# Bf16 expert sums, late tiles in the dead transposed-x room, and another instruction order, in a fused local-attention and expert kernel

## Chip, cores, metric

The kernel runs on one core of one Trainium2 chip. The metric is device time in microseconds (us) for one execution. "Span" is the time from the first to the last instruction in a profiled execution; it is about 1.7 us shorter than the time. Engines: PE is TensorE, DVE is VectorE, ACT is ScalarE, POOL is GpSimd, SP is SyncE (here only a queue of DMA issues, "SPq"). Runs are "fast" or "slow"; a slow one is over 1.5% above the fastest of the same kernel. The "granted clock" is the share of its full clock that PE was allowed, and "DMA share" the mean busy share of the core's 16 DMA engines.

## The reference, cut to what matters

```python
x  = A_x                                   # 2048 tokens x 640, bf16
xn = layernorm(x)
q, k, v = split(xn @ wqkv)                 # 32 heads of 20
# each token attends to 8 keys: itself and 2, 4, ..., 14 tokens back
logits = einsum("bhsd,bhswd->bhsw", q, k[idx]) * scale      # masked where idx < 0
s  = einsum("bhsw,bhswd->bhsd", softmax(logits), v[idx]) @ wo
r  = xn @ w_r;  top 2 tokens by r go through an expert:
y  = (silu(x_sel @ w_gate) * (x_sel @ w_up)) @ w_down * sigmoid(r_sel)
g  = silu(xn with the two y's added at their tokens)
return x + s * g
```

## The kernel before

The 2048 tokens are four blocks of 512, j = 0 to 3. The work is cut into some 470 named steps, and a long string, ORDER, is the program order in which they are emitted. Each engine's own instructions come out near that order; the framework puts in the semaphores. Names that matter here: `xjg` is DVE's product q*k for block j from group g on (one group 4096 elements per partition, 2.29 us; two groups 8192, 4.4 us), `rjg` PE's reduction of it, `yjg` DVE's product attn*v, `ojgu` PE's reduction of that, `lb ex dn lg sb at` the softmax chain of PE and ACT, `s` output projections, `cm` DVE's combine with the gate, `od` POOL's accumulating store, `vs` the store of v, `vl` the gathers of shifted v, `kh` the key halo copy, `xr` the load of the last block's residual rows, `zo zw zi` the gate tiles' way through DRAM, `*` the 128x32 tiled form of a PE step (four times as many PE instructions), F4 a filler.

```python
k_sb = big.tile([P, KD, HALO + 2 * ST], BF)        # per group: 14 halo columns, even block, odd block

def key_halo():                                     # ACT: the odd block's last columns become the halo
    nc.scalar.copy(k_sb[:, :, 0:HALO], k_sb[:, :, 2 * ST:2 * ST + HALO])

def qk(j, gs):                                      # DVE: n groups at once
    koff = g * (HALO + 2 * ST) + HALO + ST * (j % 2)
    kv = bass.AP(k_sb.tensor, k_sb.offset + koff,
                 [[k_sb.ap[0][0], P], [HALO + 2 * ST, n], [-DIL, W], [1, ST]])
    nc.vector.tensor_tensor(out=dst, in0=q_sb[...].to_broadcast([P, n, W, ST]), in1=kv, op=ALU.mult)

def ss_tile(j):                                     # two rooms in turn for four blocks of s
    acc["ss", j] = ring.tile([P, TPS, D], BF, tag="ss", bufs=2)

def load_res():                                     # the last block's residual rows
    acc["xr"] = xr = ring.tile([P, TPS, D], BF, tag="we", name="xr")
    nc.sync.dma_start(xr[:], x2[ST * (NST - 1):S, :]...)

def gate_back():                                    # gate tiles back from DRAM, SyncE's queue too
    for k in range(2):
        dst, src = gate_tile(k)
        nc.sync.dma_start(out=dst, in_=src)

def expert_in(k):                                   # sums for the sigmoid, fp32 operands
    for i in range(2):
        nc.tensor.matmul(hp[:, FB:FB + 1], lhsT=srow[:, i, :], rhs=t8[:, i:i + 1], ...)
# ... (cut)
```

Of the kernel before, what the change touches and what calls it, by code (L numbers as in the profile page):

```python
# [8 lines left out]
BF = mybir.dt.bfloat16  # L9
F32 = mybir.dt.float32  # L10
# [45 lines left out]
x00d bh br x01d in x02d ls00 wq wk x03d ls01 W ls02 ls03 lv03 xd3 lv01 lp02 lp03 lz02 bi lz03 lp00 t02 lp01 te02  # L56
xd1 bn lz00 t03 lz01 te03 t01 ls32 t00 te01 q01b wv ls12 te00 q00b q01be k04 q00be q02a xd2 ls31 k00 q00a bm
q02ae k04e ls13 q04 mu3 mg5 ls11 k00e pr2 pr1 q00ae ls10 mg6 mg2 xw ls20 bs q03 ls33 lv33 lv31 q04e v02 ls30
q03e lp1 v02e v00 lz10 lz11 v01 lz12 v04 ls21 q02b v01e v00e lz13 t10 v03 k02 v04e x00 lv21 q02be te10 k01 ls23
v03e t12 k02e t13 r00 t11 vs0 k01e k03 te12 te13 lv23 x04 q01a ls22 lp3 lz31 te11 k14 q12 q01ae lp2 k11 lz32  # L60
k03e k10 k13 x02 lz22 k12 t22 q14 t31 q12e k11e k14e k10e k13e k12e q14e x03 x01 lz21 lz33 vh1 r01 te22 r02 lz20
r03 te31 vl01 vl02 r04 lb0 wc q13* q13e kh mg1 mu4 t33* mx0 mg3 v12 te33 ml0 t32 ng0 v12e lz30 x12 v14 t21 te32
ex0 vl00 lz23 q11 te21 v14e t20 te20 dn0 x11 q10 mg7 mu2 t23 q11e lg0 t30 sb0 v11 q10e v10 te23 v13 te30 q21 at0
x10 rt pr0 q22* r10 v11e v10e v13e m8 mi k21* r11 q23* vs1 g21 q22e g00 k23* g11 q21e k21e r12 k32* y00 k24* rr
g01 rm q23e mg4 lb1 o001 y01 k32e o001e vh2 o000 k24e q20* y02 mx1 k23e v20* k20* mg0 ix o011 v20e h0 q24* q20e
mu1 mu0 o011e ml1 k20e k22* hs o020 ng1* h1 v24* q24e o010 o000e wo1 wo3 k22e g10 wo2 k30* md1 md0 md4 x22 v22*
hb ex1 k30e x20 v24e dn1 k31 x21 lg1 o020e sb1 md2 v22e md3 k31e at1 wo0 v23 ht q30 v21 g31 v21e r20 q31* v23e
vs2 q33* g20 q31e g30 vl10 r21 q32* vl11 q30e y10 o010e r22 q33e q32e v33* o100 lb2 o101 q34* k33* vh3 mx2 v31*
q34e o101e hc ml2 k33e v31e y11 ng2* ex2 o100e o110 vl12 v32* v32e dn2 v34* vl20 lg2 sb2* at2 vl21 yp x30 y12
o111 zo r30 v33e zr v34e v30 s04 s03 v30e s02 vl22 x31 s01 s03e s00 s04e vs3 s01e o110e k34 zw o120 k34e s02e  # L70
o111e y20 o120e r31 xr x32 o200 s10* r32 zi y21 s12* s13* s00e vl30 lb3 mx3 ml3 y22 o200e vl31 cm0 ng3* s10e
s13e o201 s11* o211 ex3 dn3 od0 o201e lg3 s12e sb3* s14* at3 s11e y30 o211e s14e o220 o210 o220e o210e y34 vl32
cm1 y31 F4 o300 s20* s24* o340 s23 F4 s22 s21 o300e s23e s24e s20e o340e s22e s21e s33a o310 y32 o320 cm2 y35
o310e o320e od1 y33 s30* o350 od2 s31* o331 o330 o350e s30e s33b cm30 o331e o330e s32 s31e s32e cm33 cm31 od30
od33 cm32 od31 od32
# [25 lines left out]
def _build(ctx, tc, nc, A_x, A_wqkv, A_wo, B_w_r, B_w_gate, B_w_up, B_w_down, out):  # L101
# [39 lines left out]
    srow = big.tile([1, 2, P], F32, name="srow")  # L141
# [327 lines left out]

    def ss_tile(j):  # L470
        if ("ss", j) not in acc:
            acc["ss", j] = ring.tile([P, TPS, D], BF, tag="ss", bufs=2, name=f"ss{j}")
        return acc["ss", j]
# [46 lines left out]
    def load_res():  # L520
        acc["xr"] = xr = ring.tile([P, TPS, D], BF, tag="we", name="xr")
        nc.sync.dma_start(xr[:], x2[ST * (NST - 1):S, :].rearrange("(c p) d -> p c d", p=P))
# [71 lines left out]
    def route_merge():  # L594
# [8 lines left out]
        nc.vector.tensor_copy(ii[:], gi[:])  # L603

# [5 lines left out]
    def expert_in(k):  # L610
        hp = bank("pj", [P, FB + 1 - k], bufs=3, name="hp")
        if k == 0:
            for i in range(2):
                nc.tensor.matmul(hp[:, FB:FB + 1], lhsT=srow[:, i, :], rhs=t8[:, i:i + 1], start=(i == 0), stop=(i == 1))
# [193 lines left out]
```

## Time and profile before

| | before |
|---|---|
| time, median of the first 3 runs | 145.85 us (144.7 to 145.99) |
| span of the profiled run | 144.1 us |
| PE, DVE, ACT busy | 129.8, 117.7, 110.3 us |
| DVE's first weighting of values of block 1 (y10) starts | 84.72 us |
| from there to DVE's last instruction | 56.5 us, of which 3.7 waits |

The prediction below shows most of this profile. Four things it did not show proved to matter. First, the stages by tens of microseconds (us, then length, busy us of PE, PEld, DVE, ACT, POOL, granted clock, DMA share, GB/s), where 40 to 60 us is an undisturbed stretch:

```profile
40.00:50.00 10.00, 9.89 (x121) 5.95 (x112) 8.87 (x4) 9.76 (x19) 1.40 (x3) 1.00 0.60 145
50.00:60.00 10.00, 10.00 (x156) 4.78 (x158) 7.99 (x5) 9.05 (x12) 0.00 (x0) 1.00 0.46 147
```

Second, the key halo copy in ACT's instructions in order of time (start, us, engine, line, operation, out<-in). There is no bracket, so it waited for nobody:

```profile
41.34 0.25 ACT L343 COPY k_sb<-k_sb 128x70 bf16<-128x70 bf16 x1
```

The DMA queue by which instructions themselves come in (packets, MB, share of 16 engines), from the page:

```profile
q8 instruction: 15, 0.25, 0.8%
```

```profile
78.70 0.33 PE L184 MATMUL lg<-ld,nsel 128*128 128x128 bf16 x3 [0.68 <-issue]
...
98.49 0.77 PE L655 MATMUL yp<-wd,hT 128*32 128x160 bf16 x26 [0.63 <-issue]
```

### The profile page before, as it was taken

The numbers are of one execution on the slowest core, as the hardware profiler recorded it, in microseconds if no ns is written. First come the engines' busy times: TensorE is split into PE (matmuls) and PEld (weight loads), VectorE is DVE, ScalarE is ACT, GpSimd is POOL, SyncE is SP. The second block draws the span as 40 slices with busy tenths as digits, with TensorE's granted clock in tenths as the row PEclk, the third lists the DMA queues.
The fourth block names the chain that finished last, engine by engine and source line by source line (L and its number), as shares of the span: only waits on it lengthen the run. The fifth ranks groups of instructions, "written<-read, shape, count | busy, mean of one in ns | idle before, by whom it ended". The sixth has DMA issues, their size and how long they took to land.

```text
span 144.1 us, 4710 instructions
## 1 busy us (share of the span) xinstructions
PE 129.8 (90%) x1998; PEld 70.5 (49%) x2008; DVE 117.7 (82%) x112; ACT 110.3 (77%) x207; POOL 40.1 (28%) x130
## 2 busy tenths in 40 slices
PE   6959899999999999999997999997999888899740
PEld 2345445554565644545554454674644564645520
DVE  0563899899599758998168999999999997797971
ACT  3897999966699979996997989879258699164350
POOL 7888000047140000235500000551405057131200
PEclk9999999999999999999999999999999999999999
DMA  4999989629996024897999995798588979949682
GB/s 139 351 376 365 473 338 337 246 81 361 238 261 166 7 102 134 294 282 177 225 235 259 258 324 184 182 235 189 152 249 255 223 174 192 219 111 168 85 193 91
DMA packets 17516, 32.18 MB, mean 223 GB/s; under 512 B 2280, under 2 KB 14760, under 8 KB 16424
## 3 DMA queue, kind: packets, MB, share of 16 engines
q0 software_dynamic: 3888, 12.72, 39.5%
q1 hardware_dynamic: 10696, 16.15, 34.9%
q10 hardware_dynamic: 2912, 3.02, 6.4%
q8 instruction: 15, 0.25, 0.8%
q14 instruction: 5, 0.04, 0.1%
HBM read 26.24 MB, written 7.61 MB: 235 GB/s over the span
## 4 chain that ended last, share of the span: by engine, by line
PE 46%; DVE 20%; ACT 16%; DMA 11%; issue 3%; SPq 1%; POOL 1%; ACTq 0%; DVEq 0%
PE pp L184 21%; DVE prod L439 10%; DVE prod L363 8%; DMA z<-in_A_x_dram 7%; PE pp L187 7%; PE so L184 6%; ACT z L539 4%; DMA vsh<-vd 4%; ACT L169 3%; PE oa L454 3%; PE lg L374 2%; PE tp L192 2%; ACT k_sb L340 2%; ACT q_sb L333 2%; ACT o_sb L464 1%
## 5 line engine op out<-in xcount | busy, mean ns | idle before, releaser
L363 DVE TENSOR_TENSOR prod<-q_sb,k_sb 128x4096 bf16<-128x4096 bf16 (+1 forms) x14 | 44.6, 3201 | 7.9 <-PE oa L454 3.5
L355 POOL DMA_DIRECT2D vsh<-vd x48 | 24.3, 549 | 81.5 <-DMA vd<-v_sb 43.1
L439 DVE TENSOR_TENSOR prod<-attn,vsh 128x8192 bf16<-128x8192 bf16 (+4 forms) x15 | 44.6, 2994 | 2.1 <-DMA vsh<-vd 1.2
L184 PE MATMUL pp<-xnT,wqkv 128*128 128x512 bf16 (+1 forms) x188 | 41.1, 362 | 0.9 <-ACT q_sb L333 0.4
L187 PE MATMUL pp<-xnT,wqkv 128*32 128x512 bf16 x480 | 28.7, 379 | 0.1
L184 PEld LDWEIGHTS <-wqkv 128*128 128x128 bf16 x195 | 18.4, 98 | 18.7 <-issue 1.4
L187 PEld LDWEIGHTS <-wqkv 128*32 128x32 bf16 x480 | 13.3, 97 | 11.8 <-issue 0.4
L464 ACT CAST o_sb<-oa 128x512 bf16<-128x512 f32 (+2 forms) x22 | 11.9, 560 | 4.2 <-PE oa L454 4.2
L281 DVE BATCH_NORM_STATS2 st<-z 128x6 f32<-128x320 bf16 x20 | 8.6, 474 | 6.5 <-DMA z<-in_A_x_dram 6.4
L454 PE MATMUL oa<-prod,sall 128*32 128x512 bf16 (+2 forms) x240 | 12.0, 309 | 2.0 <-DVE prod L439 1.1
L333 ACT ACTIVATE q_sb<-pp 128x512 bf16<-128x512 f32 (+1 forms) x23 | 12.2, 543 | 2.0 <-PE pp L184 2.0
L340 ACT CAST v_sb<-pp 128x512 bf16<-128x512 f32 x20 | 11.4, 586 | 2.8 <-PE pp L184 1.7
L340 ACT CAST k_sb<-pp 128x512 bf16<-128x512 f32 x20 | 11.5, 590 | 2.6 <-PE pp L184 2.6
L169 ACT ACT_TABLE_LOAD x9 | 11.5, 1283 | 2.3 <-PEq L792 1.7
L487 ACT CAST ss<-so 128x512 bf16<-128x512 f32 x12 | 7.0, 596 | 7.0 <-PE so L184 7.0
L320 ACT COPY xnT<-tp 128x640 bf16<-128x640 bf16 x16 | 10.6, 696 | 0.4 <-PE tp L192 0.4
L374 PE MATMUL lg<-prod,ind 128*32 128x512 bf16 x160 | 10.6, 380 | 0.0
L539 ACT ACTIVATE z<-z 128x1280 bf16<-128x1280 bf16 x8 | 10.1, 1274 | 0.5 <-ACT v_sb L340 0.5
L184 PE MATMUL so<-wo,o_sb 128*128 128x512 bf16 (+1 forms) x54 | 8.9, 320 | 0.2 <-issue 0.2
L184 PEld LDWEIGHTS <-o_sb 128*128 128x128 bf16 x75 | 6.0, 98 | 6.0 <-ACT o_sb L464 0.6
L187 PEld LDWEIGHTS <-o_sb 128*32 128x32 bf16 x340 | 7.0, 97 | 4.0 <-ACT o_sb L464 0.7
L187 PE MATMUL so<-wo,o_sb 128*32 128x128 bf16 (+1 forms) x260 | 8.6, 281 | 0.0
(117 smaller groups left out, 140.5 us busy)
## 6 DMA issues: line engine op xcount, KB each, us to landing
vsh<-vd POOLq DMA_DIRECT2D x32, 262.6 KB, 5.4
vd<-v_sb ACTq DMA_DIRECT2D x4, 657.5 KB, 4.9
wqkv<-in_A_wqkv_dram SPq DMA_DIRECT2D x3, 800.0 KB, 13.1
wu<-in_B_w_up_dram SPq DMA_DIRECT2D x5, 432.0 KB, 4.1
vsh<-vd POOLq DMA_DIRECT2D x16, 131.1 KB, 6.6
z<-in_A_x_dram SPq DMA_DIRECT2D x3, 640.0 KB, 10.8
out_dram<-in_A_x_dram SPq DMA_DIRECT2D x3, 640.0 KB, 9.0
wd<-in_B_w_down_dram SPq DMA_DIRECT2D x4, 480.0 KB, 12.2
```

What stands on the lines that cost most here:

```text
L169: nc.scalar.preload_act_table_set(name)
L184: nc.tensor.matmul(dst, lhsT=lhsT, rhs=rhs, start=start, stop=stop, **kw)
L187: nc.tensor.matmul(dst[32 * c:32 * (c + 1)], lhsT=lhsT[:, 32 * c:32 * (c + 1)], rhs=rhs, start=start, stop=stop, tile_position=(0, 32 * c) ...
L333: nc.scalar.activation(out=dst, in_=pp[:], func=ACT.Copy, scale=SCALE)
L340: nc.scalar.copy(dst, pp[:])
L355: nc.gpsimd.dma_start(vsh[32 * i:32 * (i + 1), 4 * g0 * VR:4 * g0 * VR + n], src)
L363: nc.vector.tensor_tensor(out=dst, in0=q_sb[:, s0:s0 + n, :].unsqueeze(2).to_broadcast([P, n, W, ST]), in1=kv, op=ALU.mult)
L374: nc.tensor.matmul(lg[32 * w4:32 * (w4 + 1), w2, :], lhsT=ind5[:, g, :], rhs=prod[:, a:a + ST], start=(g == 0), stop=(g == G5 - 1), tile_p ...
L439: nc.vector.tensor_tensor(out=dst, in0=attn[:, :, t0:t0 + n].unsqueeze(2).to_broadcast([P, 2, 4 * ng, n]), in1=vv, op=ALU.mult)
L454: nc.tensor.matmul(oa[32 * dd:32 * (dd + 1), i, :], lhsT=sall[:, 0:32], rhs=prod[:, a:a + n], start=(w2 == 0), stop=(w2 == 1), tile_positi ...
L464: nc.scalar.copy(o_sb[:, s0:s0 + m, t0:t0 + n], acc.pop(("o", j, g, t0))[:])
L539: nc.scalar.activation(out=z[:, 2 * h:2 * h + 2, :], in_=z[:, 2 * h:2 * h + 2, :], func=ACT.Silu)
```

## The change

The intent: make the two sigmoid sums bf16 (fp32 multiplies are dearer on PE); put the s tiles of blocks 2 and 3 and the residual rows into the transposed x, which is dead after the last projection, so that they need not wait for the stores of blocks 0 and 1; drop one of two fillers; and use another order throughout. The diff, cut to its core:

```diff
 ORDER = """
-... lb0 wc q13* q13e kh mg1 mu4 t33* mx0 ... x12 ... x11 ... at0 x10 rt pr0 ...          (cut)
-... x22 v22* hb ex1 k30e x20 v24e dn1 k31 x21 ...                                        (cut)
+... q14* x11 x10 te30 kh te23 mg4 lb0 v11* ... ex0 ... lg0 sb0* rt v12e ...              (cut)
+... x20 h1 v24* v22e q24e o020 ... hb q30e x22 k31 ht ... x21 r21 hc y10 ...             (cut)
 """
-    srow = big.tile([1, 2, P], F32, name="srow")
+    srow = big.tile([1, 2, P], BF, name="srow")
+    t8b = big.tile([1, 2], BF, name="t8b")
+    def late_room(n):
+        return xnT[:].rearrange("p k s -> p (k s)")[:, n * TPS * D:(n + 1) * TPS * D]...
     def ss_tile(j):
-            acc["ss", j] = ring.tile([P, TPS, D], BF, tag="ss", bufs=2, name=f"ss{j}")
+            acc["ss", j] = ring.tile(...) if j < 2 else late_room(j - 2)
     def load_res():
-        acc["xr"] = xr = ring.tile([P, TPS, D], BF, tag="we", name="xr")
+        acc["xr"] = xr = late_room(2)
+        nc.vector.tensor_copy(t8b[:], t8[:, 0:2])
-                nc.tensor.matmul(hp[:, FB:FB + 1], lhsT=srow[:, i, :], rhs=t8[:, i:i + 1], ...)
+                nc.tensor.matmul(hp[:, FB:FB + 1], lhsT=srow[:, i, :], rhs=t8b[:, i:i + 1], ...)
```

More of the change, by code (lines that the diff above doesn't have):

```diff
@@ L55 @@
 ORDER = """
-x00d bh br x01d in x02d ls00 wq wk x03d ls01 W ls02 ls03 lv03 xd3 lv01 lp02 lp03 lz02 bi lz03 lp00 t02 lp01 te02
-xd1 bn lz00 t03 lz01 te03 t01 ls32 t00 te01 q01b wv ls12 te00 q00b q01be k04 q00be q02a xd2 ls31 k00 q00a bm
-q02ae k04e ls13 q04 mu3 mg5 ls11 k00e pr2 pr1 q00ae ls10 mg6 mg2 xw ls20 bs q03 ls33 lv33 lv31 q04e v02 ls30
-q03e lp1 v02e v00 lz10 lz11 v01 lz12 v04 ls21 q02b v01e v00e lz13 t10 v03 k02 v04e x00 lv21 q02be te10 k01 ls23
-v03e t12 k02e t13 r00 t11 vs0 k01e k03 te12 te13 lv23 x04 q01a ls22 lp3 lz31 te11 k14 q12 q01ae lp2 k11 lz32
@@ L61 @@
-k03e k10 k13 x02 lz22 k12 t22 q14 t31 q12e k11e k14e k10e k13e k12e q14e x03 x01 lz21 lz33 vh1 r01 te22 r02 lz20
-r03 te31 vl01 vl02 r04 lb0 wc q13* q13e kh mg1 mu4 t33* mx0 mg3 v12 te33 ml0 t32 ng0 v12e lz30 x12 v14 t21 te32
-ex0 vl00 lz23 q11 te21 v14e t20 te20 dn0 x11 q10 mg7 mu2 t23 q11e lg0 t30 sb0 v11 q10e v10 te23 v13 te30 q21 at0
-x10 rt pr0 q22* r10 v11e v10e v13e m8 mi k21* r11 q23* vs1 g21 q22e g00 k23* g11 q21e k21e r12 k32* y00 k24* rr
-g01 rm q23e mg4 lb1 o001 y01 k32e o001e vh2 o000 k24e q20* y02 mx1 k23e v20* k20* mg0 ix o011 v20e h0 q24* q20e
@@ L66 @@
-mu1 mu0 o011e ml1 k20e k22* hs o020 ng1* h1 v24* q24e o010 o000e wo1 wo3 k22e g10 wo2 k30* md1 md0 md4 x22 v22*
-hb ex1 k30e x20 v24e dn1 k31 x21 lg1 o020e sb1 md2 v22e md3 k31e at1 wo0 v23 ht q30 v21 g31 v21e r20 q31* v23e
-vs2 q33* g20 q31e g30 vl10 r21 q32* vl11 q30e y10 o010e r22 q33e q32e v33* o100 lb2 o101 q34* k33* vh3 mx2 v31*
-q34e o101e hc ml2 k33e v31e y11 ng2* ex2 o100e o110 vl12 v32* v32e dn2 v34* vl20 lg2 sb2* at2 vl21 yp x30 y12
-o111 zo r30 v33e zr v34e v30 s04 s03 v30e s02 vl22 x31 s01 s03e s00 s04e vs3 s01e o110e k34 zw o120 k34e s02e
@@ L71 @@
-o111e y20 o120e r31 xr x32 o200 s10* r32 zi y21 s12* s13* s00e vl30 lb3 mx3 ml3 y22 o200e vl31 cm0 ng3* s10e
-s13e o201 s11* o211 ex3 dn3 od0 o201e lg3 s12e sb3* s14* at3 s11e y30 o211e s14e o220 o210 o220e o210e y34 vl32
-cm1 y31 F4 o300 s20* s24* o340 s23 F4 s22 s21 o300e s23e s24e s20e o340e s22e s21e s33a o310 y32 o320 cm2 y35
-o310e o320e od1 y33 s30* o350 od2 s31* o331 o330 o350e s30e s33b cm30 o331e o330e s32 s31e s32e cm33 cm31 od30
-od33 cm32 od31 od32
+x00d x02d in x01d bh ls00 W x03d ls01 bi bm br lv01 ls02 ls03 lv03 lp02 lp03 bs lz02 xd1 lp00 t02 lp01 te02 lz03
@@ new lines @@
+lz00 lz01 t03 t00 wq t01 te03 te00 q01b ls10 q02b wv te01 ls11 q04 ls12 xd3 q01be v01 q02a ls13 q04e q02be lp1
+wk bn v01e mg7 q02ae ls31 v02 ls32 lv31 q00a q00ae v03 q00b lz12 lz11 v02e pr0 mg2 lz13 v03e lz10 q00be mg0 ls33
+k00 k00e v00 v00e q03 t10 k02 q03e ls30 q01a te10 k01 k02e q01ae lv33 t13 k03 t12 k04 xd2 mg6 mg3 t11 x00 k01e
+mu3 mu0 te13 lp3 k03e te12 te11 v04 k11 k04e ls20 x03 k14 k10 v04e q10 xw mg1 x01 vs0 ls23 k14e q11 k11e pr1 x02
+k13 k10e ls21 q13 q11e lv21 ls22 k12 vl02 lz33 t33 q10e k13e mg5 mu4 q12 lv23 x04 lz30 r00 wc q13e r01 r02 lp2
@@ new lines @@
+lz22 lz31 t22* r03 k12e lz32 lz23 te33 lz20 lz21 t30* t23* q12e r04 te22 vh1 q14* x11 x10 te30 kh te23 mg4 lb0
+v11* q14e mx0 vl01 vl00 t32 t31 v11e t21 ml0 ng0 v13 t20 te32 te31 te21 ex0 v12 v13e dn0 v10* te20 lg0 sb0* rt
+v12e v14* m8 v10e r10 r11 mi at0 x12 k22 g21 g11 k32 v14e rr g20 k32e pr2 k23 q21 k22e g10 rm q21e k20 k23e vs1
+q22 ix k21 q22e r12 h0 y00 o001 q20* k21e lb1 k20e mu1 y01 y02 o000 q20e mx1 mu2 wo3 wo1 o000e v23* vh2 o010 wo2
+ml1 q24* v22* md0 o001e v23e hs md1 o011 ng1* k24* g01 x20 h1 v24* v22e q24e o020 q30* o010e k24e ex1 vl10 dn1
@@ new lines @@
+wo0 md4 vl12 q23 lg1 sb1 k30 v21 hb q30e x22 k31 ht v20 md2 q23e o011e o020e v24e k30e at1 md3 v21e k31e g00 r20
+v20e vs2 vl11 q33* x21 r21 hc y10 k33* y11 g30 v33* r22 q31* g31 zo q33e o100 o101 k33e lb2 s00* mx2 q31e o100e
+y12 ml2 q32* ng2* q32e s00e o111 vh3 ex2 v33e v30* v32* dn2 lg2 v34* x30 sb2* yp v30e v32e o101e at2 v34e vl20
+o110 vl22 vl21 v31* r30 x31 k34 s04 zr s03 v31e vs3 zw s01 k34e zi s04e s02 q34 o120 y20 s03e o110e q34e r31
+o120e o111e s02e s01e x32 s13* r32 lb3 s12* xr o201 s10* s12e y21 mx3 ml3 o200 ng3* vl30 o200e ex3 s11* dn3 y22
@@ L76 @@
+lg3 cm0 sb3* o201e s10e at3 s14* vl31 s13e s11e o210 o220 o211 o210e s14e vl32 o220e y30 o211e cm1 F4 s20 s22
+s23 s22e od0 s21 od1 o300 y31 s24* y34 s23e o310 y32 o320 o340 s21e o300e s20e s24e y35 o310e o320e s31 s30 o350
+s31e o340e cm2 y33 o350e s33a* s30e cm31 o331 od31 s33b* o330 o330e o331e cm30 s32 s32e cm33 od2 od30 od33 cm32
+od32
 """
@@ L468, in outproj_mm @@
             mm4(dst, o_sb[:, o_slot(j, g), P * c:P * (c + 1)], wo[:, g, n0:n1], g == 0, g == G5 - 1)
+    def late_room(n):
+        return xnT[:].rearrange("p k s -> p (k s)")[:, n * TPS * D:(n + 1) * TPS * D].rearrange("p (c d) -> p c d", c=TPS)
     def ss_tile(j):
         if ("ss", j) not in acc:
-            acc["ss", j] = ring.tile([P, TPS, D], BF, tag="ss", bufs=2, name=f"ss{j}")
+            acc["ss", j] = ring.tile([P, TPS, D], BF, tag="ss", bufs=2, name=f"ss{j}") if j < 2 else late_room(j - 2)
         return acc["ss", j]
@@ L613, in expert_in @@
             for i in range(2):
-                nc.tensor.matmul(hp[:, FB:FB + 1], lhsT=srow[:, i, :], rhs=t8[:, i:i + 1], start=(i == 0), stop=(i == 1))
+                nc.tensor.matmul(hp[:, FB:FB + 1], lhsT=srow[:, i, :], rhs=t8b[:, i:i + 1], start=(i == 0), stop=(i == 1))
         for k5 in range(KD):
```

## The prediction

> **What bounds the kernel now.** I read the page first: the busy shares, then the chain that ended last, then the groups. Then the chain in order of time, VectorE's (DVE) instructions in order of time, and the table of stages.
>
> ```profile
> PE 129.8 (90%) x1998; PEld 70.5 (49%) x2008; DVE 117.7 (82%) x112; ACT 110.3 (77%) x207; POOL 40.1 (28%) x130
> ...
> PE 46%; DVE 20%; ACT 16%; DMA 11%; issue 3%; SPq 1%; POOL 1%; ACTq 0%; DVEq 0%
> ```
>
> See that no engine alone is the bound: PE is busy 90% of the span, DVE 82%, and the chain changes between them. The rows of stages say where (us, then busy us of PE, PEld, DVE, ACT, POOL, then clock, DMA share, GB/s):
>
> ```profile
> 76.00:89.00 13.00, 12.27 (x171) 6.09 (x161) 12.96 (x3) 11.68 (x19) 0.00 (x0) 1.00 0.99 264
> 89.00:109.00 20.00, 19.11 (x365) 11.10 (x365) 19.81 (x8) 13.64 (x24) 5.80 (x12) 1.00 0.78 202
> 109.00:120.00 11.00, 10.01 (x298) 6.28 (x289) 10.46 (x5) 9.53 (x17) 4.21 (x9) 1.00 0.86 215
> 120.00:130.00 10.00, 8.77 (x180) 4.76 (x178) 8.83 (x5) 5.30 (x11) 4.39 (x6) 1.00 0.86 167
> 130.00:141.20 11.20, 7.77 (x173) 4.43 (x172) 9.23 (x13) 4.72 (x12) 1.29 (x1) 1.00 0.81 141
> ```
>
> From 76 us on DVE is full: 12.96 of 13.00, then 19.81 of 20.00, and only after 109 us does it wait. So whatever starts the long DVE run earlier, or takes a DVE wait out of the tail, comes off the end; PE has little room beside it. The tail waits of DVE, from its instructions in order of time:
>
> ```profile
> 109.12 2.29 DVE L363 TENSOR_TENSOR prod<-q_sb,k_sb 128x4096 bf16<-128x4096 bf16 x1 [0.30 <-ACT k_sb L340]
> ...
> 119.77 2.29 DVE L439 TENSOR_TENSOR prod<-attn,vsh 128x4096 bf16<-128x4096 bf16 x1 [0.42 <-ACT attn L432]
> 123.22 2.29 DVE L439 TENSOR_TENSOR prod<-attn,vsh 128x4096 bf16<-128x4096 bf16 x1 [1.17 <-DMA vsh<-vd]
> ...
> 131.06 1.49 DVE L514 TENSOR_TENSOR ss<-ss,z 128x2560 bf16<-128x2560 bf16 x1 [0.81 <-ACT ss L487]
> ...
> 139.25 0.49 DVE L527 TENSOR_TENSOR ss<-ss,z 128x640 bf16<-128x640 bf16 x1 [0.73 <-ACT ss L510]
> ```
>
> With 0.29 before the last tile's L529 these are 3.7 us. The stretch from DVE's first weighting of values for the second token block (84.72, "y10" below) to its last instruction (141.19) is 56.5 us: 52.8 of work, 3.7 of waits. After it come 2.9 us for the last store, to the span's 144.1. The last multiply on PE (137.38 to 138.9) waits for DVE's last product too, so the end is a DVE chain with one PE step in it.
>
> The start is DMA: DVE sits idle for its second batch of x, PE does not.
>
> ```profile
> 13.00 0.89 DVE L281 BATCH_NORM_STATS2 st<-z 128x6 f32<-128x320 bf16 x2 [3.18 <-DMA z<-in_A_x_dram]
> ...
> 71.53 2.29 DVE L363 TENSOR_TENSOR prod<-q_sb,k_sb 128x4096 bf16<-128x4096 bf16 x1 [3.47 <-PE oa L454]
> ...
> 76.04 8.76 DVE L363 TENSOR_TENSOR prod<-q_sb,k_sb 128x8192 bf16<-128x8192 bf16 x2 [1.38 <-ACT k_sb L340]
> ```
>
> The second and third lines are the middle: DVE loses 3.47 + 1.38 us just before the full stretch begins, waiting for PE to free the product buffer and for ACT to bring k.
>
> **What the Trainium skill says.** (1) "FP8 and Floating Point Precision", TensorE Precision Notes: true FP32 takes 4 passes through the array. This trace agrees that fp32 is dearer: the two sigmoid-sum matmuls stand as four of 250 ns with four weight loads of 185 ns, where bf16 loads take 97; from 67.20 to the next group's 67.73 they hold PE 0.5 us. (2) "TensorEngine Tiling (Array Packing)", Key Properties: changing the tiling mode drains TensorE. The trace shows a small cost: eight 128x32 matmuls between untiled work occupy 0.55 us where the same eight, inside tiled work, take 0.43. (3) "DMA: Bandwidth & Descriptors", Anatomy of one DMA: about 2.0 us plus bytes / 436e3. For 640 KB that is 3.5 us; this trace's accumulating stores land after 6.6, so contention counts, and I use 6.6. (4) "TensorE: Matmul & The Clock Gate", Part 1: the clock is gated after about 3.4 us of idleness. Here the clock is 1.00 in every row and PE's longest wait after the first 10 us is about 0.7 us; one filler of four matmuls less won't cool it.
>
> **The change, part by part.**
>
> Fp32 to bf16 sums: PE saves about 0.4 us (0.5 less two one-column bf16 matmuls); DVE gains one copy, 0.16 us by the row of its like (157 ns). Weight: 0.2 to 0.4 us, at 60 to 70 us where PE is full.
>
> One filler gone: 4 x 0.216 = 0.87 us of PE, but fillers sit where PE would wait for DVE's results anyway. Weight: near 0.
>
> Late s tiles and row gathers in the dead transposed x: the third and fourth s tile waited for the first two tiles' accumulating stores. Those start at 119.65 and 127.22; with 6.6 us they land at 126.3 and 133.8. The first writes into the reused tiles start at 127.42 and 134.17. So the ring was satisfied by 1.1 and 0.4 us: alone the new room is worth nothing, but it takes away a floor under any earlier tail, and lets the two stores be issued later (the order puts the last value gather of block 3 before both; before, the first store stood ahead of it).
>
> The order. In it I follow three things, from the instruction lists and the row durations.
> Start: x block 1 is fetched ahead of the q weights. In the trace the queue lands in order at about 0.37 MB/us (640 KB after 1.9 us, 800 KB after 2.1). x block 1 then lands near 8.6 instead of 14.9 and the q weights near 10.8 instead of 9.0. PE, which starts projecting at 10.45, loses 0.3 to 0.4; DVE's 3.18 + 0.75 us vanish and its first q*k product (22.70) comes near 20.7.
> Middle: the router's matmuls stand 2.2 us of PE work earlier (46.9 to 44.7 in PE's queue, summed with 0.216 us per matmul of 512), the one 4096-wide product of block 2 is no longer first, so the 3.47 us wait on PE goes; the next one waits about 1.2 for q block 3 instead. Adding rows, y10 starts near 82.5: 2.2 earlier. It can't start sooner, as it needs the product half that PE's reduction "r20" frees, which stands at the same 75.4 us of PE work in both orders.
> Tail: PE's queue is the same to 0.1 us at these points (81.9 before o100, 105.6 before mx3), so PE gives about 1 us (the sums above and fewer stalls). I expect 1.3 us of new wait before x31 (its buffer is freed by "o110", moved behind the expert's last matmuls, 86.5 to 91.4 in PE's queue) and 0.3 before x32. Then y30 starts near 118.2 instead of 119.77, the value gather wait shrinks from 1.17 to about 0.5 since a 2.2 us product and a combine now stand before it, and the 0.81 at the third combine goes (it stands one product later). Final wait 0.3 to 0.7.
> Sum: 82.5 + 52.8 + (1.3 + 0.3 + 0.5 + 0.5) = 137.9, plus 2.9 for the store = 140.8, against 144.1: 3.3 us. Such sums omit stalls that nobody foresees (the trace has 0.68 and 0.63 us of "issue" on PE), so I take 0.5 off: 2.8.
>
> **Rivals.** (a) PE takes the bound back. For: it has the same work, less 1.3 us, and was full to 109 us; if PE reaches o100 no earlier than 89.2, DVE's head start is eaten by waits for buffers, and only the tail's gain, 1 to 1.5 us, is left: about 144.5. Against: from 64 to 89 us PE falls 1.4 us behind its own summed work (64.38 against 58.5, 89.19 against 81.9). (b) The start turns round: q weights after x, with 0.8 MB of v and x behind, hold PE until 11.5; everything is 1 us later: about 144. For: landing times are my arithmetic. (c) ACT becomes the wait: four 1.17 us gates and a 1.28 us table load now stand in one row near 50 to 57 us, with projections waiting in three banks to be emptied. My walk has PE waiting less than 0.5 there; 2 us would make it 145. (d) The value gathers and both stores now come together after 115 us; if a gather takes 8 instead of 5.6 us, its wait stays 1.2 or more: plus 1.
>
> **Range and chances.** 145.85 - 2.8 = 143.0. Everything good gives 4.5 less (141.3), two rivals together give 145. The 2% line is at 142.9, where my middle lies, so the first two outcomes are nearly even; rivals pull to the slow side. Slower by 2% would need an unseen wait of 5 us.
>
> **What would show it.** DVE's first product near 20.7 and no x wait at 10 to 13 us; the clock 1.00 throughout; fp32 matmul rows gone; y10 near 82.5; o100 near 88; new wait before x31 about 1.3; third combine without a wait; DVE waits from y10 on near 2.6 in sum. Wrong would be: PE idle over 1 us at 10 to 13 or 50 to 62 us, y10 later than 84, or value gathers over 7 us in the tail.

## The result, and the profile after

The changed kernel takes 155.37 us (median of 4, 154.01 to 157.78); before, in the same rounds, took 145.92. The ratio is 1.0622, 95% interval 1.0496 to 1.0748: slower by 6%. A ratio here is the mean time of one kernel's fast runs over that of the other's fast runs of the same rounds, so it is not quite the ratio of the medians quoted. The profiled execution was the slowest of the four (157.8 us, span 156.0); the granted clock, 0.956, is like that of the others (0.962 to 0.965). The three fast runs left no profile; k2c below, nearly the same program and profiled in a fast run (155.8 us), shows the same waits.

The page after: the busy shares, the granted PE clock in 40 slices, and the chain that ended last, by engine:

```profile
PE 132.6 (85%) x1956; PEld 71.1 (46%) x1966; DVE 118.2 (76%) x113; ACT 110.8 (71%) x207; POOL 40.9 (26%) x130
...
PEclk9999999999995569999999999999999999599999
...
PE 48%; ACT 29%; DVE 8%; DMA 6%; issue 5%; ACTq 1%; SPq 1%; DVEq 0%
```

The work is nearly the same (busy times grow by 2.8 us on PE, by 0.5 on DVE and ACT), but the clock falls to about half in two places and DVE's share of the chain has gone from 20% to 8%, ACT's from 16% to 29%. The stages of the changed kernel say where:

```profile
40.00:50.00 10.00, 4.75 (x140) 2.69 (x133) 9.78 (x7) 1.50 (x4) 2.53 (x4) 0.86 1.04 241
50.00:60.00 10.00, 7.44 (x77) 4.76 (x81) 0.44 (x1) 7.74 (x14) 0.00 (x0) 0.63 0.37 82
```

Set them beside the same rows of before. From 40 to 50 us ACT is busy 1.50 instead of 9.76 and PE 4.75 instead of 9.89; from 50 to 60 DVE is busy 0.44 instead of 7.99. One after the other stood still. The instructions of ACT, PE and DVE there, in order of time (the bracket is the idle time just before the instruction and what ended it):

```profile
50.52 0.25 ACT L344 COPY k_sb<-k_sb 128x70 bf16<-128x70 bf16 x1 [7.92 <-DVE prod L364]
...
51.26 1.03 ACT L387 ACTIVATE ef<-lg 128x1024 bf16<-128x1024 f32 x1
```

```profile
52.34 0.40 PE L393 MATMUL den<-ef,sall 128*32 128x128 bf16 x8 [7.59 <-ACT ef L387]
```

```profile
41.67 8.76 DVE L364 TENSOR_TENSOR prod<-q_sb,k_sb 128x8192 bf16<-128x8192 bf16 x2 [0.22 <-PE lg L375]
61.70 0.70 DVE L588 MAX8 top<-rp 128x8 f32<-128x512 f32 x1 [11.27 <-PE rp L583]
...
92.80 10.96 DVE L440 TENSOR_TENSOR prod<-attn,vsh 128x8192 bf16<-128x8192 bf16 x3 [0.84 <-issue]
```

Read them as one chain. DVE runs two products of block 1 from 41.67 to 50.43. ACT's quarter-microsecond halo copy waits 7.92 us for the second. Behind it in ACT's queue stands the exp of block 0; PE waits 7.59 us for that; then DVE waits 11.27 us for the router's logits, which PE computes behind. y10 starts at 92.80 instead of 84.72: 8.1 of the 11.9 us by which this span is longer.

The other 3.8 us are lost in the tail. PE stops within a group of 80 small multiplies, in "issue"; DVE then waits in more places than before:

```profile
127.42 1.05 PE L188 MATMUL so<-wo,o_sb 128*32 128x128 bf16 x61 [0.34 <-ACT ss L491]
131.11 0.46 PE L188 MATMUL so<-wo,o_sb 128*32 128x128 bf16 x19 [2.64 <-issue]
```

```profile
133.16 1.49 DVE L518 TENSOR_TENSOR ss<-ss,z 128x2560 bf16<-128x2560 bf16 x1 [1.55 <-ACT ss L493]
135.77 6.23 DVE L440 TENSOR_TENSOR prod<-attn,vsh 128x4096 bf16<-128x4096 bf16 x4 [1.12 <-DMA vsh<-vd]
...
152.10 0.49 DVE L531 TENSOR_TENSOR xnT<-xnT,z 128x640 bf16<-128x640 bf16 x1 [1.72 <-ACT xnT L514]
```

From y10 to DVE's end (153.11) are 60.3 us; all waits in it are 0.77 + 0.37 + 1.08 + 1.55 + 1.12 + 0.42 + 0.30 + 1.72 = 7.3, against 3.7 before; the work, 53.0, is nearly the 52.8 of before.

### The profile page after: what moved, and what is told of

It reads as the page before. It is cut to its first block, busy times and chain, and to the rows that moved or that the text cites.

```text
span 156.0 us, 4621 instructions
## 1 busy us (share of the span) xinstructions
PE 132.6 (85%) x1956; PEld 71.1 (46%) x1966; DVE 118.2 (76%) x113; ACT 110.8 (71%) x207; POOL 40.9 (26%) x130
## 4 chain that ended last, share of the span: by engine, by line
PE 48%; ACT 29%; DVE 8%; DMA 6%; issue 5%; ACTq 1%; SPq 1%; DVEq 0%
PE pp L185 18%; DVE prod L364 7%; ACT z L543 6%; DMA wqkv<-in_A_wqkv_dram 6%; PE so L185 6%; PE pp L188 5%; PE so L188 4%; ACT o_sb L465 4%; ACT L170 4%; PE oa L455 3%; ACT k_sb L341 3%; ACT v_sb L341 3%; PE tp L193 2%; PE lg L375 2%; PE sl L185 2%
## 5 line engine op out<-in xcount | busy, mean ns | idle before, releaser
L185 PE MATMUL pp<-xnT,wqkv 128*128 128x512 bf16 (+1 forms) x208 | 46.0, 369 | 2.3 <-DMA wqkv<-in_A_wqkv_dram 1.4
L185 PEld LDWEIGHTS <-wqkv 128*128 128x128 bf16 x215 | 20.5, 99 | 22.6 <-issue 2.1
L188 PE MATMUL pp<-xnT,wqkv 128*32 128x512 bf16 x400 | 24.4, 379 | 0.5 <-ACT q_sb L334 0.5
L188 PEld LDWEIGHTS <-wqkv 128*32 128x32 bf16 x400 | 10.8, 97 | 9.9 <-issue 0.7
L455 PE MATMUL oa<-prod,sall 128*32 128x512 bf16 (+2 forms) x240 | 12.6, 317 | 0.8 <-ACT o_sb L465 0.8
L188 PE MATMUL so<-wo,o_sb 128*32 128x128 bf16 (+1 forms) x260 | 9.1, 281 | 3.0 <-issue 2.6
L185 PEld LDWEIGHTS <-o_sb 128*128 128x128 bf16 x85 | 7.0, 100 | 7.3 <-ACT o_sb L465 0.9
L188 PEld LDWEIGHTS <-o_sb 128*32 128x32 bf16 x300 | 6.2, 97 | 6.8 <-issue 3.3
L588 DVE MAX8 top<-rp 128x8 f32<-128x512 f32 x1 | 0.7, 699 | 11.3 <-PE rp L583 11.3
```

The source lines that it names most:

```text
L185: nc.tensor.matmul(dst, lhsT=lhsT, rhs=rhs, start=start, stop=stop, **kw)
L188: nc.tensor.matmul(dst[32 * c:32 * (c + 1)], lhsT=lhsT[:, 32 * c:32 * (c + 1)], rhs=rhs, start=start, stop=stop, tile_position=(0, 32 * c) ...
L455: nc.tensor.matmul(oa[32 * dd:32 * (dd + 1), i, :], lhsT=sall[:, 0:32], rhs=prod[:, a:a + n], start=(w2 == 0), stop=(w2 == 1), tile_positi ...
```

## The experiments

Theory 1: the halo copy's wait is the main loss, and it is a clash of address ranges, not of data. The products read columns 512 on of each group, the copy writes columns 0 to 13; but written for five groups with one instruction the copy spans from group 0's first column to group 4's fourteenth, and over a product of two groups lies the next group's halo. Theory 2: PE's "issue" stalls are late blocks of PE's own instructions. Rivals: the later landing of the q weights at the start; ACT's row of gates and exps as a limit of its own; the new rooms; the new order of DVE's products as such.

Eighteen kernels ran, all correct. Line numbers differ by a few between kernels. Times are medians; "before" is the kernel before in the same rounds.

| run | this, us | before, us | ratio, fast runs (95%) |
|---|---|---|---|
| k1_halo_first | 150.85 | 145.16 | 1.0402 (1.0342 to 1.0463) |
| k2b_no_range_clash | 150.86 | 145.16 | none given |
| k2c_split_copy_only | 156.33 | 145.16 | 1.0766 (1.0676 to 1.0856) |
| k3_old_order | 150.54 | 145.16 | 1.0287 (1.0217 to 1.0356) |
| k5_old_order_rows_late | 147.69 | 145.98 | 1.0077 (1.0046 to 1.0109) |
| k6_loads_later | 152.29 | 145.98 | 1.0308 (1.0205 to 1.0412) |
| h1_new_head_old_tail | 154.95 | 145.98 | none given |
| h2_old_head_new_tail | 145.74 | 145.98 | 1.0008 (0.9977 to 1.0038) |
| k4_before_halo_late | 147.35 | 145.50 | 1.0145 (1.0060 to 1.0229) |
| k7_fewer_pe_instructions | 148.50 | 145.50 | 1.0225 (1.0155 to 1.0295) |
| h3_old_start_new_rest | 149.39 | 145.50 | 1.0258 (1.0159 to 1.0358) |
| k9_still_fewer | 147.10 | 146.00 | 1.0068 (0.9991 to 1.0145) |
| b1_swap_on_h2 | 144.95 | 146.00 | 0.9910 (0.9853 to 0.9966) |
| b2_swap_and_untiled | 146.44 | 146.00 | 1.0024 (0.9971 to 1.0078) |
| c1_k9_rows_later | 145.70 | 146.02 | 0.9992 (0.9965 to 1.0019) |
| c2_b1_untiled | 144.36 | 146.02 | 0.9879 (0.9830 to 0.9929) |
| c3_b1_untiled_rows_later | 143.87 | 146.02 | 0.9869 (0.9818 to 0.9920) |
| d1_before_swap_only | 145.71 | 145.59 | 0.9996 (0.9966 to 1.0026) |

### The halo copy: k1, k2b, k2c, k4

```diff
 k1:  -... q14* x11 x10 te30 kh te23 ...
      +... q14* kh x11 x10 te30 te23 ...
 k2c: -nc.scalar.copy(k_sb[:, :, 0:HALO], k_sb[:, :, 2 * ST:2 * ST + HALO])
      +for g in range(KD):
      +    nc.scalar.copy(k_sb[:, g, 0:HALO], k_sb[:, g, 2 * ST:2 * ST + HALO])
 k2b: as k2c, and  +XU[1] = XU[0]      # block 1's products one group at a time: x12 x13 x10 x11 ... x14
 k4 (on the kernel before):  -... q13* q13e kh mg1 ... at0 x10 rt ...
                             +... q13* q13e mg1 ... at0 x10 kh rt ...
```

> Only the key halo copy is moved, ahead of both of block 1's two-group q*k products. Theory (the 7.9 us wait of ScalarE's halo copy for VectorE's second product is the cause: softmax, PE's den and the router stand behind it): that wait is under 0.5 us, PE's wait before den under 1 us, VectorE's wait before the router's top-8 under 3, the clock 1.00 from 40 to 60 us, y10 starts near 84 instead of 92.8, and the time is 145.5 to 147.5 (8 to 10 below the changed kernel). Rival A (the start with q weights late, plus the tail, are what cost): the time stays above 151. Rival B (ScalarE's row of gates and exps is the limit in the middle): the halo wait goes but PE still waits over 3 us between 45 and 62 us.

> The halo copy stays where the changed kernel has it, but is split into five copies of one group each, and block 1's products are made one group at a time, so no address range of a product covers the columns that the halo copy writes. Theory (the wait is between address ranges, not data: the products read columns 512 on, the copy writes columns 0 to 13): the halo copies wait under 0.5 us for VectorE, and the time is within 1.5 us of k1_halo_first (two more products, 0.2 us each, and four more small copies, about 0.2 us each). Rival (a true need of the products, or the place in ScalarE's queue as such): about 155, as the changed kernel.

> Only half of the former: the halo copy is split into five copies of one group, block 1's products keep two groups each. Theory: the copy for group 1 still falls into the range of the product of groups 0 and 1 (it spans from group 0's column 512 to group 1's end), so the wait of 7 to 8 us stays and the time is 154 to 157. Rival (it is the copy's own width over five groups that clashes): the wait goes, 146 to 148.

> The kernel before with one step moved: the key halo copy stands behind the last two-group q*k product of block 1 in program order, instead of ahead of all of them. Theory: it now waits for that product (which ends near 52 us), and what ScalarE has behind it comes later: a wait of 1 to 5 us of ScalarE for VectorE at the halo copy, and 1 to 4 us more in all: 147 to 150. Rival (the wait hurts only in the new order): the wait is there, but the time stays within 1 us of before.

The halo copy in ACT's instructions in order of time, first in k1, then k2b, k2c and k4:

```profile
40.87 0.25 ACT L344 COPY k_sb<-k_sb 128x70 bf16<-128x70 bf16 x1
```

```profile
41.56 0.62 ACT L345 COPY k_sb<-k_sb 128x14 bf16<-128x14 bf16 x5
```

```profile
41.60 0.21 ACT L345 COPY k_sb<-k_sb 128x14 bf16<-128x14 bf16 x1
49.58 0.51 ACT L345 COPY k_sb<-k_sb 128x14 bf16<-128x14 bf16 x4 [7.76 <-DVE prod L365]
```

```profile
51.45 0.25 ACT L343 COPY k_sb<-k_sb 128x70 bf16<-128x70 bf16 x1 [2.39 <-DVE prod L363]
```

In k1 and k2b nothing is waited for. In k2c the first of the five copies (group 0) goes at once and the second (group 1) waits 7.76 us: its columns lie inside the span of the product of groups 0 and 1. k2b differs from k2c only in that the products have one group each, and the wait is gone, though the copies stand at the same place of the order. So theory 1 holds in its exact form: it is the range, not the data, nor the place as such. Of the same rounds, the fast runs of k2c have a mean of 155.99 us (three), of k2b 149.37 (two; its other two are slow, so its median in the table is not used) and of k1 150.79 (four): the wait costs 6.6 us against k2b and 5.2 against k1. In the profiles y10 comes 6.0 us earlier in k1 (86.26) than in k2c (92.29). Eight to ten were expected of k1, and 145.5 to 147.5 us; 150.85, just under the 151 of rival A, is a miss, as are y10 (84 expected) and the clock (0.50 from 46.8 to 50.2 us): there is a second cause. k4 shows the same from the other side: the step moved in the kernel before brings 2.39 us of ACT's wait and 1.45% (2.1 us; at least 0.6% by the interval), as expected.

### The new rooms: k3, k5

k3 is the changed kernel's code with the old order; k5 moves one step in it, `xr`, from ahead of to behind `zi`.

```diff
 k3:  the changed kernel's code, ORDER of before
 k5:  -... r31 xr x32 o200 s10* r32 zi y21 ...
      +... r31 x32 o200 s10* r32 zi xr y21 ...
```

> All of the changed kernel's code (bf16 sigmoid sums, late s tiles and residual rows in the dead x) with the old order, both fillers kept. Theory from the prediction: 0.2 to 0.4 us less from the sums, nothing from the room: 145.2 to 146.2, the same as before within 0.5 us. Rival A (the room itself saves waits in the tail): 144.5 or less. Rival B (the room brings new waits, as its writers must wait for the last readers of x, or the bf16 copy on VectorE costs): above 147.

> As k3_old_order, but the load of the residual rows stands behind the two reads of the gate tiles in SyncE's queue instead of ahead of them. Theory: in k3_old_order these rows, now going into the dead x, waited 4.3 us for the last projection that reads x, and held up the gate tiles behind them, for which VectorE's first combine then waited 4.9 us; so here that wait is under 0.6 us and the time 144.8 to 146.2, equal to before within 0.5%. Rival (the late s tiles in x or the bf16 copy cost by themselves): the wait stays or moves to another combine, 148 or more.

SyncE's queue in order of time, first before, then k3 (the load of the residual rows, then the gate tiles' way back), and what DVE's first combine waited for in k3:

```profile
104.89 0.41 SPq L522 DMA_DIRECT2D xr<-in_A_x_dram  x1
106.19 5.12 SPq L688 DMA_DIRECT2D z<-zd  x2
```

```profile
108.75 0.42 SPq L526 DMA_DIRECT2D xnT<-in_A_x_dram  x1
110.06 7.66 SPq L693 DMA_DIRECT2D z<-zd  x2
```

```profile
123.52 1.49 DVE L518 TENSOR_TENSOR ss<-ss,z 128x2560 bf16<-128x2560 bf16 x1 [4.89 <-ACT o_sb L465]
```

The bracket names ACT's o_sb, which had ended by 122.86; the instruction also waits for the gate tiles, and those were late. In its new room the residual load must wait for the last projection that reads x (4.3 us in the queue's own waits), and the gate tiles stand behind it. The prediction had checked the s tiles' room and not this one. k3 (fast runs 148.64 and 149.65) refutes "the code is worth 0.2 to 0.4 us"; with `xr` behind `zi` (k5) the 4.89 us wait is gone and of the 2.9% only 0.8% is left. Its profile, of a slow run, has PE "issue" stalls of 1.22, 1.45 and 0.42 us where before has 0.68 and 0.63; that they make the 0.8% is not shown. In the new order `xr` stands behind `zi` anyway, so this cause has no part in the changed kernel's 155 us.

### Which half: h1, h2, h3, and the loads: k6

h1 is k1's order up to y10, then the old one; h2 the old order up to y10, then the new one; h3 the same with the cut at y00, 29 us earlier (55.71 and 84.72 in before). All have the changed code and `xr` behind `zi`. k6 is k1 with three loads moved from 33 us to behind the router's.

```diff
 k6:  -... vs0 ls23 k14e q11 k11e pr1 x02 ... q10e k13e mg5 mu4 q12 ...
      +... vs0 ls23 k14e q11 k11e x02 ... q10e k13e q12 ... mi mg5 mu4 ... pr2 pr1 ...
```

> The changed kernel's code; its order (with the halo copy first) up to the second block's weighting of values, then the old order, with the residual rows behind the gate tiles as in k5. Theory (the remaining 5 us of k1_halo_first are half in the head, PE's stall at 43.5 us, half in the tail, PE's stall at 122 us and what follows): 147 to 148.8. If all is in the tail: 145 to 146.5. If all is in the head: 149.5 or more.

> The counterpart: the changed kernel's code, the old order up to the second block's weighting of values, the new one from there. Theory (half and half): 147 to 148.8, with PE's stall of 1.5 to 2.7 us near 120 us in the 80 small multiplies, and VectorE's waits after its start of the second block's weighting at 5.5 to 7 us in sum (3.7 before). Rival (the new tail is sound and only suffers from the head's delay and its DMA): 144 to 145.5, waits 3 us or less, as the prediction had it.

> The changed kernel's code; the old order up to the first block's weighting of values (y00), the new one from there (the cut 27 us earlier than in h2). Theory (the new middle and tail are sound where the loads and gathers of the old start stand): y00 near 55.7 as before, y10 near 82.5, the time 142.5 to 145. Rival (PE can't follow an earlier y10, or its instruction stalls take it back): 145 to 147.

> As k1_halo_first, with three loads (one 640 KB residual copy, two weight parts) moved from the burst at 33 to 36 us to behind the router's, near 57 us. Theory: PE's 2.7 us 'issue' stall at 43.5 us is a fetch of its own instructions that queues behind that burst; here it is under 1 us, and the time 1.5 to 3 us below k1_halo_first: 147.8 to 149.4. Rival (the fetch queues behind the twelve value gathers, which stay): the stall stays above 2 us and the time within 0.7 us of k1_halo_first.

h2 is equal to before (1.0008): the new tail loses nothing where it is reached as the old head reaches it. That is the rival of "half and half", though a little above its 144 to 145.5, and its waits after y10 are 3.1 us, not 2.6. h1 was slow in three of four runs (154 to 157) and 149.72 in the one fast run, with PE "issue" stalls of 3.77, 1.37, 1.83 and 2.37 us in the profiled, slow one. h1 is too unsteady for a number, but it doesn't contradict h2: most of what is wrong comes with the head. k6 did not do what its edit says: of the three loads only the residual copy moved to 57 us, the two weight parts still went out near 34 us. The stall stayed (2.94 us, in a slow run) and the time too (two fast runs, 149.42 and 151.06), so the residual copy isn't its cause; the value gathers may be, but k6 alone does not show that. h3 missed: no stall over 0.5 us and no halo wait, yet 149.4. Its spliced middle brings waits of its own; DVE waited 3.67 us for the expert's second matmul, and y10 came at 87.81, not 82.5:

```profile
78.56 0.67 DVE L638 SCALAR_TENSOR_TENSOR hb<-hs,sg,hp 128x432 bf16<-128x432 f32 x1 [3.67 <-PE hp L626]
```

### PE's own instructions: k7, k9

In k1 the halo wait is gone, and PE stalls at the same place for another reason. PE's instructions in k1, and the stage behind (columns as above):

```profile
43.54 0.23 PE L393 MATMUL den<-ef,sall 128*32 128x128 bf16 x3
46.50 0.28 PE L393 MATMUL den<-ef,sall 128*32 128x128 bf16 x5 [2.74 <-issue]
```

```profile
48.00:50.00 2.00, 1.78 (x15) 1.44 (x14) 1.92 (x1) 1.96 (x4) 0.00 (x0) 0.50 1.12 235
```

A group of eight multiplies is cut after the third by 2.74 us, and the clock then falls to 0.50. A group can't wait in its middle for data it already used. Counting PE's instructions in the built kernels explains it:

| kernel | stall ended at, us | length, us | matmuls left in the group | number of the next PE instruction |
|---|---|---|---|---|
| changed kernel | 131.11 | 2.64 | 19 of 80 | 3266 = 194 + 12 x 256 |
| k1 | 46.50 | 2.74 | 5 of 8 | 706 = 194 + 2 x 256 |
| k1 | 124.22 | 2.27 | 19 of 80 | 3266 |
| k5 | 99.89 | 1.22 | 24 of 64 | 2498 = 194 + 9 x 256 |
| k5 | 122.33 | 1.45 | 18 of 80 | 3266 |
| k5 | 127.70 | 0.42 | 26 of 80 | 3522 = 194 + 13 x 256 |
| h1 | 133.61 | 2.37 | 20 of 80 | 3522 |

I found 29 PE "issue" stalls of over 0.35 us in the twenty profiles (from 8 us on), and all 29 lie at such a number, whatever the work there. Most such crossings pass without one: there are about 15 in a kernel. (In before and k4 the list has to be corrected by six instructions: the two fp32 multiplies stand in it as two and in the trace as four matmuls and four weight loads.) The page's queue q8 brought 15 blocks with 0.25 MB in all; 3,945 instructions in blocks of 256 are about 15. In k1 the one q8 packet near the first stall falls between 43.5 and 44 us, at a DMA share of 1.0, and PE goes on at 46.5. The first line here is k1 from 43.5 to 44 us; the second is from the page of k9 (below), which has 671 PE instructions fewer, and with them three blocks fewer:

```profile
q8 instruction: 1, 0.02, 15.4%
...
q8 instruction: 12, 0.20, 0.6%
```

So PE ran out of instructions, and the next block came late. The traces say more: at each of the 29 stalls PE goes on 2.3 to 2.9 us after the start of one q8 packet, which itself took 0.9 to 1.4 us. The packet started between 2.3 us before and 0.9 us after PE stopped, and that makes a stall short or long. The DMA share was 0.94 or more in 27 of the 29; in the other two (0.76 in h1, 0.27 in b2) PE went on 2.4 and 2.3 us after the packet, so between a full and a less full DMA lie at most 0.6 us of this time. What starts a packet late is not shown.

If so, fewer PE instructions for the same work should help, without a change in DMA. k7 removes the `*` from four steps near 41 us in k1; k9 from thirteen more.

```diff
 k7:  -t22* ... t30* t23* ... q14*      +t22 ... t30 t23 ... q14
 k9:  also  q24* v22* ng1* k24* v24*  q32* ng2* v30* v32* v34* sb2*  sb3* s14*   without the star
```

> As k1_halo_first; only three groups of transposes and one projection near 41 us are made in the untiled form (a quarter of the PE instructions, the same data and DMA). So PE has 120 instructions fewer there and every later boundary of 256 instructions falls on other work: the one that stalled in the 'den' group at 43.5 us falls 120 instructions later in time, the one in the 80 small multiplies at 122 us falls into untiled work. Theory (PE stalls at each 256th instruction when the next block of its instructions comes late): the stalls of 2.7 and 2.3 us at those places are gone, at most 1.5 us of such stalls remains elsewhere, and the time is 2.5 to 5 us below k1_halo_first: 146 to 148.5. Rival (the stalls come with the place, the small multiplies, or with DMA load as such): stalls of over 2 us at the same work, time within 1 us of k1_halo_first.

> As k7_fewer_pe_instructions, with thirteen more groups of PE work (projections, group sums, output projections between 68 and 126 us) in the untiled form. Theory (what keeps k7 3 us above before is late instruction blocks, 2.15 us at 75.9 and 1.22 us at 104): PE's 'issue' stalls over 0.3 us sum to less than 1 us, the changes of form cost 0.5 to 1.5 us on PE, and the time is 145.5 to 147.5. Rival (the order itself, its start and its middle, is slower by 3 us): the stalls go and the time stays at 148 to 149.5.

In k7 both stalls are gone from their places. Two others have come at the next boundaries that fell into dense work, 8 matmuls before a group's end (instruction 1474) and 10 (2498):

```profile
75.90 0.62 PE L187 MATMUL pp<-xnT,wqkv 128*32 128x512 bf16 x8 [2.15 <-issue]
104.08 0.82 PE L374 MATMUL lg<-prod,ind 128*32 128x512 bf16 x10 [1.22 <-issue]
```

k7 takes 148.5, 2.35 below k1 (of other rounds; the ratios to before, 1.0402 and 1.0225, differ by 1.8%, 2.6 us): the edge of what was expected, since 3.4 us of stalls remained and not 1.5. In k9 no stall over 0.2 us is left, and two of its DVE instructions tell the rest:

```profile
82.59 10.96 DVE L439 TENSOR_TENSOR prod<-attn,vsh 128x8192 bf16<-128x8192 bf16 x3 [0.83 <-issue]
...
125.48 6.23 DVE L439 TENSOR_TENSOR prod<-attn,vsh 128x4096 bf16<-128x4096 bf16 x4 [3.13 <-DMA vsh<-vd]
```

y10 starts at 82.59, as the prediction had it (82.5), once both the halo wait and the late blocks are out. This also settles two rivals: k9 has the changed kernel's row of gates and exps on ACT and its rooms, so neither holds y10 up. The time, 147.1 (fast runs 146.8), is inside the range expected, and its ratio is 1.6% below that of k7, 2.3 us; but now a value gather is waited for.

### The tail's gather, and a version that beats both: c1, b1, b2, c2, c3, d1

c1 is k9 with the residual load issued from ACT's queue behind `at3` (at 117.6 us) instead of SyncE's (113.8 us), since DVE first reads it near 135 us. b1 is h2 with one swap: block 2's two-group product ahead of the one-group product, the part of the new middle that the prediction counted on. b2, c2 and c3 add untiled steps, c3 also the later residual load. d1 is the swap alone, in the kernel before.

```diff
 b1 (on h2) and d1 (on before):  -... md4 x22 v22* hb ex1 k30e x20 v24e ...
                                 +... md4 x20 v22* hb ex1 k30e x22 v24e ...
 b2:  -sb3* s14*      +sb3 s14
 c2:  also q32* ng2* v30* v32* v34* sb2* without the star
 c1, c3:  -nc.sync.dma_start(xr[:], ...)      +nc.scalar.dma_start(xr[:], ...)     and xr behind at3
```

> As k9_still_fewer; only the load of the residual rows (640 KB) is issued from ScalarE's queue behind its last attn step (about 120 us) instead of from SyncE's at 114 us. Theory (it shares the DMA with the gathers for groups 1 and 2 of block 3): VectorE's gather wait of 3.1 us falls to 0.5 to 1.5 and the time is 1 to 2.5 us below k9_still_fewer: 144 to 145.5. Rival (the eight gathers alone fill the DMA): the wait stays above 2.5, 146 to 147.

> As h2_old_head_new_tail (145.74) with one swap: block 2's product of groups 0 and 1 ahead of that of group 4, as the changed kernel has it. Theory (the prediction's middle step is right in itself: the first product no longer waits 3.0 us for PE): the wait is under 0.5 us, y10 starts 1.5 to 2.5 us earlier (near 82.5), and the time is 143.5 to 145, up to 1.5% below before. Rival (PE can't keep up, buffers come free no earlier): y10 earlier by under 0.7 us, or waits of the same size after it; 145.3 to 146.

> As b1_swap_on_h2, with the group sum and the 80 small multiplies near 119 to 121 us untiled (120 PE instructions fewer there). Theory: PE's late instruction block there (0.5 us in h2) goes, and the time is 0.1 to 0.6 us below b1; rival: it only moves, or the change of form costs as much: within 0.2 us of b1 or above.

> As b1_swap_on_h2, with k9's eight untiled groups from 85 us on. Theory: late instruction blocks in the tail sum to under 1 us (3.3 + 0.9 in b1's profiled run), no slow runs by such a stall, 143.8 to 145.2; rival: the changes of form cost more on PE than they save, 145.5 or more.

> As c2_b1_untiled with the residual rows later as in c1. If the rows delay the gathers, 0.3 to 1.5 us below c2 (143.3 to 144.8), as the gather waits there are 0.5 to 1.3 us; if not, equal to c2 within 0.4 us.

> The kernel before with one swap: block 2's q*k product of groups 0 and 1 ahead of that of group 4. If the swap is all that counts: y10 2 to 2.6 us earlier than before (82.2 to 82.8), 143.9 to 145.2, as b1. Rival (the gain reaches the end only with the new tail, since the old tail's accumulating stores put a floor under it, the s tiles being reused 1.1 and 0.4 us after them): y10 earlier all the same, but VectorE's waits in the tail grow by 1 to 2 us and the time is within 0.7 us of before.

c1: the gather wait falls from 3.13 to 0.31 us and the time to 145.70, equal to before. One late block is left in its profile (PE stood 1.06 us before 131.17). The share of that step is not exact: k9 and c1 ran in different rounds, and their ratios differ by 0.8%, 1.1 us. b1: the wait of 3.0 us that h2 has ahead of block 2's first product is 0.46, and y10 starts at 82.36 in place of h2's 84.94:

```profile
68.22 4.43 DVE L363 TENSOR_TENSOR prod<-q_sb,k_sb 128x8192 bf16<-128x8192 bf16 x1 [0.46 <-ACT k_sb L340]
...
82.36 4.42 DVE L439 TENSOR_TENSOR prod<-attn,vsh 128x8192 bf16<-128x8192 bf16 x1 [2.17 <-ACT v_sb L340]
```

The fast runs are 0.9% below before; the profiled run was a slow one (148.3), with a 3.30 us stall at instruction 3266. b2 cleared that place, but a later boundary then fell into the last microseconds (1.33 us at 131.84), and the gain was lost: a miss. c2 and c3 kept boundaries out of the dense tail: 144.36 and 143.87, ratios 0.9879 and 0.9869; none of their 12 runs is slow, where b1 and b2 have 2 of 6 each. c3 is the fastest of all, 1.3% below before; that it beats c2 isn't shown, as the intervals overlap.

d1 gained nothing (0.9996). In its profiled run, one of its fastest (144.88), y10 is 1.4 us earlier (83.32; 2 to 2.6 expected), and the tail's waits are no larger than before's (0.42, 1.11, 0.81, 0.73 us), so the mechanism that I had named for the rival, larger waits, is not seen, though its time came true. Why the swap pays on h2 and not on before stays open (the two intervals just touch, at 0.9966).

## Why the prediction was wrong

**The start.** Half right. The x waits at 10 and 13 us went; 2.00 us came at 15.53 for the last block, and DVE's first product began at 21.43 (20.7 predicted). PE waited 1.41 us for the q weights to 11.55; the prediction had 0.3 to 0.4, and "PE idle over 1 us at 10 to 13" was one of its signs of being wrong. In k1 and k9 the same order has DVE's first product at 20.3 to 20.4, so this part varies by 1 us between executions. It isn't the cause: c1, with the same start, equals before.

**The middle is the step that failed.** "The router's matmuls stand 2.2 us of PE work earlier" is true of PE's queue, and "adding rows, y10 starts near 82.5" summed PE and DVE. Rival (c) looked at ACT only from 50 to 57 us, and only at its gates: "My walk has PE waiting less than 0.5 there." It never asked what each instruction in ACT's queue waits for. The halo copy, 0.25 us of work, had been put behind two products whose range it touches. It waited 7.92 us, and y10 came at 92.80. Without it k1 and k2b are 5.2 and 6.6 us faster than k2c. "Slower by 2% would need an unseen wait of 5 us" was right, and this was that wait. The number predicted for y10 was sound once this wait and the late instruction blocks were out: 82.59 in k9. The built list of the changed kernel, which was to be had before predicting, shows a DVE semaphore at this copy that before does not have.

**The clock "1.00 throughout" was wrong too.** The clause "PE idle over 1 us at ... 50 to 62 us" as a sign of a wrong prediction did fire: PE stood 7.59 us before den (44.75 to 52.34), and the clock was 0.50 from 47.1 to 57.4 us, with the eight `lg` matmuls at 1.06 us (0.61 in before). It was this wait, and not the missing filler, that the fall followed.

**"Such sums omit stalls that nobody foresees ... so I take 0.5 off" was mis-sized.** In the changed kernel the one such stall is 2.64 us, in k1 two of 5.0 in sum, in h1 four of 9.3. Their places are not random: each stands at a 256th PE instruction. Taking them out was worth about 2.6 us (k1 to k7) and 2.3 us (k7 to k9) by the ratios to before, and the halo wait had hidden one of them: k2c has no such stall, k2b one of 2.71 us just there.

**The rooms.** "Alone the new room is worth nothing" overlooked that the residual rows moved too. Under the old order this cost most of 2.9% (k3); under the new one, with `xr` behind `zi`, it did not arise.

**The tail.** Waits after y10 were predicted at 2.6 us. Measured: 7.3 in the changed kernel; 3.7 even in c3 (1.28 before the two-group product of block 3, 0.37, 0.30, 1.71). The 1.3 us before x31 was well sized (0.77 in the changed kernel, 1.30 in k9 and c1), the gather's 0.5 was 1.12. The last wait, predicted at 0.3 to 0.7, is 0.30 + 1.72: this is the term that no experiment removed. So the tail is the second step that failed: in c1, the change's own order with the halo wait and nearly all late blocks out, y10 is 2.0 us earlier than before (82.73), but the waits after it are 5.6 us where 2.6 were predicted and before has 3.7. The one eats the other, and c1 only equals before, where 2.8 us were predicted.

**The sums in bf16** were right: the two multiplies stand at 72.60 and 72.72 us, 0.12 apart, where before they held PE 0.53; 0.4 us of PE, in a stretch that did not bound this kernel.

Adding up, by the ratios to before in each one's own rounds: changed kernel 1.0622, k1 1.0402, k7 1.0225, k9 1.0068, c1 0.9992. The steps are 2.2% (halo), 1.8% and 1.6% (late instruction blocks) and 0.8% (gather), or 3.2, 2.6, 2.3 and 1.1 us, each uncertain by about 1%. The halo's step is smaller here than against k2c, which is itself slower than the changed kernel (1.0766). What stays open: why the first value gathers fall into a fuller DMA in the new order, what starts the instruction blocks late, and the gap between d1 and b1.

## What to carry to other kernels

Before trusting a reordered program, go through the short instructions too, and read for each one which engine's semaphore it waits for: a copy of 0.25 us cost 5 to 7 us in runs of the same rounds, because an access pattern's span, not its elements, decided whom it waited for. Count the instructions as well as the work: where a tiled form makes four instructions of one, PE can outrun the arrival of its own program, and the untiled form of some groups then wins although PE was no less busy (130.1 us in k7, 130.8 in k9). A room that is "dead" is dead only after its last reader, and whatever stands behind its first writer in the same queue waits with it.

## What the Trainium skill lacked or had wrong

- "Runtime: NRT & Kernel Launch", Instruction fetch mechanics: it says that instructions come in 16 KiB blocks of 256, that the next is fetched while the current one runs, and that crossing a boundary is "mostly hidden". The block size agrees (15 blocks, 0.25 MB; all 29 stalls at multiples of 256 from instruction 194). "Mostly hidden" holds by count (29 stalls at some 290 crossings in twenty profiles), but the page gives no size for one that isn't hidden: 0.4 to 3.8 us here.
- "TensorE: Matmul & The Clock Gate", Part 1: about 3.4 us of idleness before the clock falls. After 7.6 us of waiting the clock did fall to 0.50; but it fell to 0.50 after stalls of 2.6, 2.7 and 2.3 us too (changed kernel, k1), and not after 2.15 us (k7) or 2.72 us (k9, before 131.17), so no single length divides them.
- No page that I read gives the price of staying tiled in instructions that have to be fetched: with 13 more groups untiled (276 matmuls fewer) PE was busy 130.8 us in k9 against 130.1 in k7, and the kernel's ratio to before was 1.6% lower.
- No page has the waiting by address range that decided here: 7.76 us for a copy of 14 columns that the product does not read (k2c), none when the product had one group (k2b).
